# Weight conversions of a second feed-forward moved into the attention, with fewer and larger transfers and a new schedule table

## The chip, the cores and the metric

One core of one Trainium2 chip runs the whole program once. The metric is the device time of that execution in microseconds (us). Engines in the profile: PE is TensorE's matmuls and PEld its weight loads, DVE is VectorE, ACT is ScalarE, POOL is GpSimd, SP is SyncE, which here only issues transfers (SPq in the rows). Each engine works through its own instructions strictly in the order in which they were written.

## The reference

Three stages follow each other, in float32 outside the weights, which come in as float64.

```python
# attention: 4 batches, 8 heads, 576 positions, head size 64
cum = np.cumsum(np.maximum(s, 0.0), axis=-1)
bias = -(cum[:, :, :, None] - cum[:, :, None, :])
scores = np.where(causal, -1000000000.0, scale * q @ k.T + np.minimum(bias, 0.0))
attn = softmax(scores);  x = attn @ v            # then (2304 tokens, 512)
# first feed-forward: d_ff 2048
h = x @ w_in;  g = np.maximum(h, 0.0) + np.log1p(np.exp(-np.abs(h)));  x = g @ w_out
# second feed-forward: d_ff 1536
xn = x / rms * rms_g;  g = xn @ w_gate;  val = xn @ w_val
out = (silu(g) * val) @ w_out
```

## The kernel before

**Weights.** A weight chunk is 128 x 512 float64 values. `w_fetch` loads it raw (512 KB, two raw buffers), `w_conv_a` (ScalarE), `w_conv_d` (VectorE, lines 257 to 262) and `w_conv_p` (GpSimd, line 268) turn its bits into float32. `w_hi` and `w_lo` then split it into a high and a low half, since each product of the feed-forwards is three matmuls (high by high, high by low, low by high; `mm3`). The first feed-forward (ph 1) has 32 chunks, the second (ph 2) 36. `w_store` puts a converted chunk into DRAM (256 KB), `w_load` fetches it back. Of the 68 chunks, 12 of ph 1 are converted and split during the attention. The other 20 of ph 1 and all 36 of ph 2 are converted during the first feed-forward: 24 of the latter are stored, 12 split at once and kept.

**Attention.** 32 heads go in 16 pairs p. For a pair: q and k are loaded (`a_load`), transposed on TensorE (`a_qt`) and split (`a_qh`, `a_ql`). A first pass of scores (`a_one`) gives row maxima on VectorE (`a_m`, line 465), which are transposed (`a_mt`, line 473, once a pair) and sent by a transfer into rows of the operand `aq` (`a_md`, lines 483 and 484). A second pass (`a_two`) makes the transposed scores with the maxima taken off, ScalarE takes exp of them (`a_e`), and `a_v` multiplies by [v | 1], so that 64 rows of the result are the output and the others the row sum. `a_ox` evacuates to xz, `a_zd` moves a sum row into z, `a_zr` makes reciprocals, `a_rd` stores them, `a_rb` broadcasts them into rb, `a_xm` multiplies on GpSimd (line 558) and `a_xw` writes x to DRAM.

**Order.** `attention_ops` lists each of these steps as an operation with an engine, a duration, what it depends on and a period (`base`). `attention_order` ranks them by base x 14 + the table `OFF`, and then repeatedly takes the one that can start first by those durations, the lowest rank first among equals. The result is one order for each engine's instructions. The conversions in it are the operations CF, CA, CD, CP, CH, CL, one chunk each `CONVR` periods. Two of the first feed-forward's products, H0 and H1, are in the same list.

**First feed-forward.** Tokens go in 6 tiles of 384, d_ff in 16 slices f; 96 steps i, the slices 0 to 5 for all tiles first. A step is 12 matmuls for h (`m1_h`), a chain over ScalarE and VectorE (`m1_abs` to `m1_gl`; e, u, l, gh and gl are its tiles), and 12 matmuls for y (`m1_y`). Steps and conversions are placed on one axis by the tables `OFF1` and `OFF2` and sorted. The pool m1 of this stage takes memory that pools of the attention held, so its first tiles wait until those are free. The second feed-forward follows in 72 steps.

Of the kernel before, what the change touches and what calls it, by code (L numbers as in the profile page):

```python
# [45 lines left out]
    "LV": -70.00,  # L46
    "QT0": -54.82,
    "QH0": 10.73,
    "QL0": -43.19,
    "QT1": -41.13,  # L50
    "QH1": -23.99,
    "QL1": -51.10,
    "AQ": -22.67,
    "RA": 33.90,
    "KA": 26.80,
    "RB": 26.23,
    "KB": 49.27,
# [36 lines left out]
    "V11": 21.91,
    "O01": 9.83,
    "O11": 65.74,
    "ZD": -7.14,
    "ZR": -70.00,
    "RS": 24.74,
    "BC": -36.84,  # L100
    "XM": -39.94,
    "XW": 60.21,
    "LD": -44.35,
    "CF": -3.51,
    "CA": -49.20,
    "CD": 59.71,
    "CP": 31.53,
    "CH": -35.20,
    "CL": 63.09,
    "XL": -61.60,  # L110
    "X0": 31.53,
    "X1": 43.56,
    "X2": 45.40,
    "X3": 46.41,
    "H0": -33.34,
    "H1": 19.94,
}
CONV0 = 0.45
CONVR = 1.15
# [34 lines left out]
def attention_moe_kernel(ctx, tc, q, k, v, s, w_in, w_out, w_gate, w_val, w_out2, rms_g, out):  # L154
    nc = tc.nc
# [18 lines left out]
    NA = 2 * FA  # L174
    STEPS = [(t, t, f) for t in range(NTILE) for f in range(FA)]
# [134 lines left out]
    def setup():  # L310
# [3 lines left out]
        for i in range(3):  # L314
            t = pools["nat"].tile([P, NB, 3, D], F32, tag=f"vn{i}", name=f"vn{i}", bufs=1)
# [719 lines left out]
```

## Time and profile before

| | |
|---|---|
| median of 3 runs | 1204.03 us (1203.38 to 1204.65) |
| the profiled execution | 1203.66 us |
| its span, first to last instruction | 1201.9 us |
| PE busy | 1125.2 us, 94% of the span |
| DVE busy | 728.3 us, 61% |
| ACT busy | 543.7 us, 45% |
| POOL busy | 420.2 us, 35% |

The attention takes the first 272 us or so, the first feed-forward the time to about 750 us, the second the rest. The shares are averages over three stages with different limits; what counts is the busy time stage by stage, and which wait ends last there. The rows for that are below.

### The profile page before, as it was taken

How to read it: one execution, taken by the hardware profiler on the slowest of the kernel's cores; microseconds unless marked ns; L12 is line 12 of the kernel's file. 1: busy time of each engine (PE TensorE's matmuls, PEld its weight loads, DVE VectorE, ACT ScalarE, POOL GpSimd, SP SyncE). 2: the span in 40 equal slices, each digit the busy share in tenths (PEclk: the TensorE clock that was granted, in tenths of full speed). 3: DMA queues.
4: the chain of work that ended last, by engine and by line, in shares of the span. 5: the costliest groups of instructions: out<-in, count | busy, mean ns of one | idle time of the engine just before them, and what ended most of it. 6: DMA issues, size and time to landing. Idle time of an engine off the chain costs nothing.

```text
span 1201.9 us, 18473 instructions
## 1 busy us (share of the span) xinstructions
PE 1125.2 (94%) x6884; PEld 1037.3 (86%) x6884; DVE 728.3 (61%) x1208; ACT 543.7 (45%) x1179; POOL 420.2 (35%) x368
## 2 busy tenths in 40 slices
PE   4999999996999989999888889999999999999998
PEld 3788888886988889998887878999999999999997
DVE  5666655415999999989999897343233332333322
ACT  1444544346777777676676756341121211212111
POOL 4434443225644543456667677660000000000000
PEclk9999999997999999999999999999999999999999
DMA  6555543224333345434533233231001010010000
GB/s 141 149 131 136 140 107 101 69 80 126 130 123 123 123 134 182 134 110 157 162 126 126 66 97 118 93 123 41 7 7 40 14 40 7 7 40 14 27 1 27
DMA packets 129018, 107.55 MB, mean 89 GB/s; under 512 B 69056, under 2 KB 114752, under 8 KB 128864
## 3 DMA queue, kind: packets, MB, share of 16 engines
q1 hardware_dynamic: 128896, 106.37, 29.6%
q8 instruction: 54, 0.88, 0.3%
q14 instruction: 36, 0.29, 0.1%
q0 software_dynamic: 32, 0.00, 0.0%
HBM read 80.36 MB, written 25.83 MB: 88 GB/s over the span
## 4 chain that ended last, share of the span: by engine, by line
PE 47%; DVE 23%; ACT 3%; issue 2%; DMA 1%; POOL 0%; DVEq 0%; SPq 0%
DVE gl L779 5%; PE v L727 4%; PE v L728 4%; PE v L729 4%; PE g L729 4%; PE g L728 4%; PE g L727 4%; DVE l L770 4%; DVE e L762 3%; PE o L903 3%; PE o L904 3%; PE o L902 3%; DVE ur L258 2%; DVE e L766 2%; DVE ur L262 2%
## 5 line engine op out<-in xcount | busy, mean ns | idle before, releaser
L268 POOL TENSOR_TENSOR wf<-ur 128x512 int32<-128x512 int32 x68 | 94.6, 1391 | 187.1 <-DVE ur L262 97.4
L728 PE MATMUL y<-gl,w 128*128 128x384 f32 x384 | 135.0, 351 | 25.5 <-DVE gl L779 25.5
L727 PE MATMUL y<-gh,w 128*128 128x384 f32 x384 | 131.7, 343 | 14.8 <-ACT e L746 11.6
L887 DVE TENSOR_TENSOR u<-g,u 128x384 f32<-128x384 f32 x71 | 39.5, 557 | 159.1 <-ACT u L886 159.1
L729 PE MATMUL y<-gh,w 128*128 128x384 f32 x384 | 131.1, 341 | 0.0
L465 DVE TENSOR_REDUCE mc<-s 128x1 f32<-128x128 f32 (+4 forms) x160 | 77.8, 537 | 68.6 <-PE s L451 47.2
L889 ACT ACTIVATE gh<-l 128x384 fp32r<-128x384 f32 x72 | 37.8, 524 | 156.0 <-DVE l L888 156.0
L728 PEld LDWEIGHTS y<-gl,w 128*128 128x128 f32 x384 | 73.6, 192 | 37.3 <-DVE gl L779 37.0
L886 ACT ACTIVATE u<-g 128x384 f32<-128x384 f32 x71 | 34.8, 490 | 151.9 <-PE g L729 151.9
L728 PE MATMUL g<-xl,w 128*128 128x384 f32 x284 | 95.5, 336 | 1.7 <-DVE xl L721 1.7
L779 DVE TENSOR_TENSOR gl<-l,gh 128x384 fp32r<-128x384 f32 x90 | 93.9, 1044 | 4.5 <-ACT gh L774 0.7
L727 PE MATMUL g<-xh,w 128*128 128x384 f32 x284 | 95.7, 337 | 0.7 <-ACT xh L720 0.7
L729 PE MATMUL g<-xh,w 128*128 128x384 f32 x284 | 95.8, 337 | 0.0
L728 PE MATMUL v<-xl,w 128*128 128x384 f32 x284 | 95.6, 337 | 0.0
L727 PE MATMUL v<-xh,w 128*128 128x384 f32 x284 | 95.5, 336 | 0.0
L729 PE MATMUL v<-xh,w 128*128 128x384 f32 x284 | 95.4, 336 | 0.0
L727 PE MATMUL h<-xh,w 128*128 128x384 f32 x256 | 87.5, 342 | 6.3 <-DVE e L766 6.3
L774 ACT ACTIVATE gh<-l 128x384 fp32r<-128x384 f32 x96 | 49.9, 520 | 92.9 <-DVE l L770 92.5
L513 ACT ACTIVATE e<-t 128x448 f32<-128x448 f32 (+2 forms) x128 | 57.2, 502 | 73.9 <-PE t L506 71.9
L728 PE MATMUL h<-xl,w 128*128 128x384 f32 x256 | 86.7, 339 | 3.8 <-POOL xl L724 3.6
L727 PEld LDWEIGHTS y<-gh,w 128*128 128x128 f32 x384 | 73.4, 191 | 17.0 <-ACT e L746 11.9
L762 DVE SCALAR_TENSOR_TENSOR e<-u,e 128x384 f32<-128x384 f32 x96 | 74.4, 775 | 21.1 <-ACT l L754 21.0
(168 smaller groups left out, 3018.2 us busy)
## 6 DMA issues: line engine op xcount, KB each, us to landing
raw<-in_moe_w_out_dram SPq DMA_DIRECT2D x28, 512.0 KB
raw<-in_moe_w_in_dram SPq DMA_DIRECT2D x16, 512.0 KB
raw<-in_moe_w_gate_dram SPq DMA_DIRECT2D x12, 512.0 KB
raw<-in_moe_w_val_dram SPq DMA_DIRECT2D x12, 512.0 KB
wf<-wf SPq DMA_DIRECT2D x24, 256.0 KB
wl<-wf SPq DMA_DIRECT2D x24, 256.0 KB
xr<-x SPq DMA_DIRECT2D x28, 192.0 KB
qn<-in_q_dram SPq DMA_DIRECT2D x32, 144.0 KB
```

Source lines behind the costliest of these rows:

```text
L268: nc.gpsimd.tensor_tensor(out=w.bitcast(I32), in0=u, in1=r3, op=ALU.add)
L465: nc.vector.reduce_max(out=o, in_=x, axis=AX.X, negate=True)
L513: nc.scalar.activation(out=st["e", p, hd][:, c:c + w], in_=st["t", p, bk][hd][:, 0:w], func=AF.Exp)
L727: nc.tensor.matmul(o, wh, xh, start=start, stop=False)
L728: nc.tensor.matmul(o, wh, xl, start=False, stop=False)
L729: nc.tensor.matmul(o, wl, xh, start=False, stop=stop)
L762: nc.vector.scalar_tensor_tensor(out=e, in0=st.pop(("u", i)), scalar=-1.0, in1=e, op0=ALU.add, op1=ALU.subtract)
L770: nc.vector.tensor_tensor(out=l, in0=l, in1=st.pop(("e", i)), op=ALU.add)
L774: nc.scalar.activation(out=gh, in_=st["l", i], func=AF.Copy)
L779: eng.tensor_tensor(out=gl, in0=st.pop(("l", i)), in1=f32(st["gh", i]), op=ALU.subtract)
L887: nc.vector.tensor_tensor(out=u, in0=g, in1=u, op=ALU.mult)
L889: nc.scalar.activation(out=gh, in_=l, func=AF.Copy)
```

## The change

All 36 chunks of the second feed-forward are now fetched, converted and stored during the attention (`CONV`, 48 chunks in all, three in about each period); during the first feed-forward 12 of them are only loaded back (`w_load`) and split. The tile `ur` of a conversion has two buffers in the attention (pool `cur`) in place of one. Transfers are merged: q and k of both heads in one each, maxima in two transfers for four, both sum rows in one, both broadcasts in one. For that both heads' outputs lie on partitions 0 to 63 (v and the ones have changed places for the second head, `vn` has a fourth column block), and `a_xm` is one operation over 64 x 1152 where there were two over 64 x 576. `OFF` has new ranks, and H0 and H1 must stand behind the last conversion. `OFF1` and `OFF2` are as before.

```diff
 OFF = {
-    "LV": -70.00,
+    "LV": -52.67,
...
-CONVR = 1.15
+CONVR = 0.33
...
+    CONV = [(1, c) for c in range(NA)] + [(2, c) for c in range(3 * F2)]
...
     def w_conv_a(ph, c):
-        ur = conv.tile([P, 2, 512], I32, tag="ur", name="ur", bufs=1)
+        pool, n = (conv, 1) if "m1" in pools else (pools["cur"], 2)
+        ur = pool.tile([P, 2, 512], I32, tag="ur", name="ur", bufs=n)
...
     def a_load(p):
-            for hd in range(2):
-                nc.sync.dma_start(out=t[:, :, hd, :], in_=src[b, h + hd].rearrange("(p r) d -> p r d", r=QR))
+            nc.sync.dma_start(out=t, in_=src[b, h:h + 2].rearrange("h (p r) d -> p r h d", r=QR))
...
     def a_md(p):
-        for hd in range(2):
-            r = slice(64 * hd + MR, 64 * hd + MR + 1)
-            nc.sync.dma_start(out=aq[r, 0:512], in_=mt[4 * hd:4 * hd + 4])
-            nc.sync.dma_start(out=aq[r, 512:S], in_=mt[8 + hd:9 + hd, 64:P])
+        r = slice(MR, 64 + MR + 1, 64)
+        nc.sync.dma_start(out=aq[r, 0:512], in_=mt[0:8])
+        nc.sync.dma_start(out=aq[r, 512:S], in_=mt[8:10, 64:P])
...
     def a_zd(p):
-        for hd in range(2):
-            nc.sync.dma_start(out=z[half(hd)], in_=st["xz", p, hd][64 - 64 * hd:65 - 64 * hd, :])
+        nc.sync.dma_start(out=z, in_=st["xz", p][64:65])
...
     def a_rb(p):
-        for hd in range(2):
-            nc.sync.dma_start(out=rb[half(hd)], in_=rdd[p][hd:hd + 1].broadcast_to([64, S]))
+        rb = st["rb", p] = pools["xo"].tile([D, 2, S], F32, tag="rb", name="rb", bufs=2)
+        nc.sync.dma_start(out=rb, in_=rdd[p].unsqueeze(0).broadcast_to([D, 2, S]))
 
     def a_xm(p):
-        for hd in range(2):
-            r = half(hd)
-            nc.gpsimd.tensor_tensor(out=x[r], in0=st.pop(("xz", p, hd))[r], in1=rb[r], op=ALU.mult)
+        x = st["x", p] = pools["xo"].tile([D, 2, S], F32, tag="x", name="x", bufs=2)
+        nc.gpsimd.tensor_tensor(out=x, in0=st.pop(("xz", p))[0:D], in1=st.pop(("rb", p)), op=ALU.mult)
...
-        for c in range(NA):
+        for c, (ph, ch) in enumerate(CONV):
...
-            cv("CA", "ACT", 0.66, w_conv_a, ["CF"] + was("CP", 1))
-            cv("CD", "DVE", 1.65, w_conv_d, ["CA"])
-            cv("CP", "POOL", 1.28, w_conv_p, ["CD"] + was("CL", 3))
-            cv("CH", "POOL", 0.62, w_hi, ["CP"])
-            cv("CL", "POOL", 1.28, w_lo, ["CH"])
+            cv("CA", "ACT", 1.33 if r3_act(ph, ch) else 0.67, w_conv_a, ["CF"] + was("CP", 2))
+            cv("CD", "DVE", 1.55 if r3_act(ph, ch) else 1.98, w_conv_d, ["CA"])
+            cv("CP", "POOL", 1.28, w_conv_p, ["CD"] + ([("CL" if c - 3 < NA else "CS", c - 3)] if c > 2 else []))
+            if ph == 1:
+                cv("CH", "POOL", 0.62, w_hi, ["CP"])
+                cv("CL", "POOL", 1.28, w_lo, ["CH"])
+            else:
+                cv("CS", "SP", 0.4, w_store, ["CP"], lat=2.2)
...
-                    for nm, fn in CONV1 + (SPLIT if ph == 1 or c < NA else (("CS", w_store),)):
+                    for nm, fn in CONV1 + SPLIT if ph == 1 else (("CF", w_load),) + SPLIT if c < NA else ():
```

What the new table does to the order shows in three places. The first is VectorE in the middle of the attention, one pair's worth: L465 (later L467) are row maxima into mc, L408 (L410) the low halves of q and k, L542 and L543 the reciprocals. Before:

```order
L465 TENSOR_REDUCE mc_165<-s 128x1 x4
L465 TENSOR_REDUCE mc_167<-s 128x2 x2
L465 TENSOR_REDUCE mc_167<-s 128x1 x2
L469 TENSOR_TENSOR mc_167<-mc_167 128x2
L465 TENSOR_REDUCE mc_167<-s 128x1 x2
L408 SCALAR_TENSOR_TENSOR hl<-qkT,hl 128x96x4
```

After, with the conversion's three steps L261, L263 and L265 on the tile ur:

```order
L467 TENSOR_REDUCE mc_165<-s 128x1 x4
L261 TENSOR_SCALAR ur<-ur 128x512
L263 TENSOR_SCALAR ur<-ur 128x512
L265 SCALAR_TENSOR_TENSOR ur<-raw,ur 128x512
L467 TENSOR_REDUCE mc_167<-s 128x2 x2
L467 TENSOR_REDUCE mc_167<-s 128x1 x2
L471 TENSOR_TENSOR mc_167<-mc_167 128x2
L261 TENSOR_SCALAR ur<-ur 128x512
L263 TENSOR_SCALAR ur<-ur 128x512
L265 SCALAR_TENSOR_TENSOR ur<-raw,ur 128x512
L467 TENSOR_REDUCE mc_167<-s 128x1 x2
L410 SCALAR_TENSOR_TENSOR hl<-qkT,hl 128x96x4
```

Two conversions now stand between groups of row maxima (a third stands between the low halves of q and those of k).

The second place is SP's queue in the middle of the attention: rd is the store of the reciprocals, rb their broadcast, aq<-mt the maxima, vn the loads of v. Before:

```order
L546 DMA rd_87<-z 128x9
L551 DMA rb<-rd_87 64x576 x2
L483 DMA aq<-mt 1x4x128
L484 DMA aq<-mt 1x16x4
L483 DMA aq<-mt 1x4x128
L484 DMA aq<-mt 1x16x4
L381 DMA vn_150<-in_v_dram 128x4x64 x2
L384 DMA vn_150<-in_v_dram 64x2x64
```

After, with the fetches of raw chunks (L240) and the store of a converted one (L275):

```order
L546 DMA rd_85<-z 128x9
L240 DMA raw<-in_moe_w_gate_dram 128x4x128
L275 DMA wf_113<-wf 128x512
L550 DMA rb<-rd_85 64x1152
L240 DMA raw<-in_moe_w_val_dram 128x4x128
L383 DMA vn_144<-in_v_dram 128x4x64 x2
L386 DMA vn_144<-in_v_dram 64x2x64
L484 DMA aq<-mt 2x4x128
L485 DMA aq<-mt 2x64
```

The maxima's transfers have moved behind a fetch and the loads of v, the broadcast behind a fetch and a store.

The third place is TensorE at the end of the attention: L524 (L525) are the last products with V, L727 to L729 (L726 to L728) the matmuls of h, of which a block has 12. Before:

```order
L727 MATMUL h<-xh,w_659 128x384
L728 MATMUL h<-xl,w_659 128x384
L729 MATMUL h<-xh,w_659 128x384
L524 MATMUL x_3768<-e,vn_144 128x192 x2
L524 MATMUL x_3768<-e,vn_144 128x64
L524 MATMUL x_3768<-e,vn_144 128x192 x2
L524 MATMUL o_3774<-e,vn_144 128x384
L524 MATMUL o_3774<-e,vn_144 128x256
L524 MATMUL o_3774<-e,vn_144 128x128
L727 MATMUL x_3840<-xh,w_945 128x384
```

After:

```order
L525 MATMUL o_4013<-e,vn_144 128x384
L525 MATMUL o_4013<-e,vn_144 128x256
L525 MATMUL o_4013<-e,vn_144 128x128
L525 MATMUL x_4021<-e,vn_144 128x192 x2
L525 MATMUL x_4021<-e,vn_144 128x64
L525 MATMUL x_4021<-e,vn_144 128x192 x2
L726 MATMUL h<-xh,w_569 128x384
L727 MATMUL h<-xl,w_569 128x384
L728 MATMUL h<-xh,w_569 128x384
```

H0 and H1 stood among the last products with V (H0 three of those further up); now both follow the last of them.

## Rows read from the trace of the kernel before

**Rows 1.** Busy time of each engine by stretch (instructions), granted clock, DMA.

```profile
core 0: us, PE busy (x) PEld busy (x) DVE busy (x) ACT busy (x) POOL busy (x), PEclk, DMA share, GB/s
...
40.00:240.00 200.00, 199.84 (x1889) 171.05 (x1888) 120.75 (x276) 93.10 (x240) 80.11 (x71) 1.00 0.45 114
240.00:284.00 44.00, 31.38 (x227) 27.32 (x223) 7.43 (x17) 17.31 (x43) 12.12 (x9) 0.89 0.30 96
284.00:440.00 156.00, 143.26 (x766) 135.33 (x767) 146.37 (x210) 116.36 (x248) 85.32 (x65) 0.98 0.40 127
440.00:480.00 40.00, 40.00 (x231) 39.75 (x230) 37.69 (x62) 31.03 (x66) 12.16 (x11) 1.00 0.50 162
440.00:730.00 290.00, 262.50 (x1441) 251.38 (x1440) 271.98 (x377) 197.89 (x412) 171.65 (x142) 0.99 0.40 128
800.00:1160.00 360.00, 360.00 (x1899) 337.56 (x1898) 114.76 (x213) 72.89 (x149) 7.01 (x5) 1.00 0.08 24
```

**Rows 2.** What PE waited for, 440 to 730 us: total, times, longest.

```profile
PE y L728 <- DVE gl L779: 14.7, 15, 3.4
PE h L727 <- DVE e L766: 5.3, 5, 1.6
PE h L728 <- POOL xl L724: 3.3, 2, 1.7
```

**Rows 3.** One short stretch, columns as in rows 1.

```profile
510.00:513.20 3.20, 3.20 (x11) 3.20 (x12) 3.13 (x6) 2.62 (x6) 1.68 (x2) 0.53 0.60 219
```

**Rows 4.** VectorE's groups, 440 to 730 us: busy us, mean ns, idle before.

```profile
L262 DVE SCALAR_TENSOR_TENSOR ur<-raw,ur 128x512 int32<-128x512 int32 x35 | 26.3, 752 | 1.2
L258 DVE TENSOR_SCALAR ur<-ur 128x512 f32<-128x512 f32 x35 | 23.9, 683 | 4.5 <-ACT ur L248 4.5
...
L260 DVE TENSOR_SCALAR ur<-ur 128x512 int32<-128x512 int32 x35 | 19.5, 558 | 1.2
```

**Rows 5.** The tile ur, 440 to 735 us: ns minimum/median/maximum, first and last start.

```profile
L248 ACT ACTIVATE ur<-raw x35: 644/656/680, 441.3 to 715.5; 128x512 f32<-128x512 f32 x35
...
L258 DVE TENSOR_SCALAR ur<-ur x35: 407/422/1514, 442.5 to 717.3; 128x512 f32<-128x512 f32 x35
...
L268 POOL TENSOR_TENSOR wf<-ur x35: 1272/1440/1612, 445.0 to 720.9; 128x512 int32<-128x512 int32 x35
```

**Rows 6.** VectorE's groups, 40 to 240 us, as rows 4.

```profile
L465 DVE TENSOR_REDUCE mc<-s 128x1 f32<-128x320 f32 (+4 forms) x140 | 68.3, 537 | 57.0 <-PE s L451 45.0 <-PE s L445 11.7
...
L262 DVE SCALAR_TENSOR_TENSOR ur<-raw,ur 128x512 int32<-128x512 int32 x11 | 7.6, 692 | 0.4
...
L258 DVE TENSOR_SCALAR ur<-ur 128x512 f32<-128x512 f32 x11 | 5.7, 522 | 0.3 <-ACT ur L248 0.3
L260 DVE TENSOR_SCALAR ur<-ur 128x512 int32<-128x512 int32 x11 | 5.6, 513 | 0.4
```

**Rows 7.** TensorE's timeline: the maxima's transpose, ten pairs apart (start, duration).

```profile
88.17 0.28 PE L473 MATMUL mT<-ident,mc 128*128 128x128 f32 x1
...
230.64 0.28 PE L473 MATMUL mT<-ident,mc 128*128 128x128 f32 x1
```

**Rows 8.** What SP's queue waited for, 20 to 240 us: total, times, longest.

```profile
SPq L483 <- ACT e L513: 12.7, 11, 3.8
SPq L483 <- ACT mt L477: 11.1, 3, 7.3
```

**Rows 9.** TensorE's timeline near the start; idle time before in brackets.

```profile
28.10 0.71 PE L392 MATMUL qkT<-ident,qn 96*128 96x96 f32 x3 [1.51 <-DMA qn<-in_q_dram]
```

**Rows 10.** TensorE's timeline at the first y.

```profile
284.05 0.66 PE L727 MATMUL y<-gh,w 128*128 128x384 f32 x1 [11.57 <-ACT e L746]
```

**Rows 11.** Timelines of SP, GpSimd and ScalarE at the attention's end.

```profile
272.91 1.10 SPq L551 DMA_DIRECT2D rb<-rd  x2
...
275.92 2.86 POOL L558 TENSOR_TENSOR x<-xz,rb 64x576 f32<-64x576 f32 x2 [5.18 <-DMA rb<-rd]
...
282.70 0.52 ACT L774 ACTIVATE gh<-l 128x384 fp32r<-128x384 f32 x1
```

More of the change, by code (lines that the diff above doesn't have):

```diff
@@ L99 @@
[L99 to L116, printed above, removed]
+    "LV": -52.67,
+    "QT0": -50.26,
+    "QH0": -14.82,
+    "QL0": -1.28,
+    "QT1": 44.67,
+    "QH1": -4.81,
+    "QL1": -59.11,
+    "AQ": -46.37,
+    "RA": -6.41,
@@ new lines @@
+    "KA": 29.15,
+    "RB": -7.55,
+    "KB": -19.97,
+    "RC": -17.34,
+    "KC": 5.02,
+    "RD": -10.66,
+    "MA0": 38.23,
+    "MA1": 27.80,
+    "MB0": -43.48,
+    "MB1": -32.64,
+    "MC0": -10.72,
+    "MC1": -70.00,
+    "MD0": 22.30,
+    "MD1": -60.64,
+    "MN": -60.28,
+    "MT": 22.32,
+    "MH": 2.98,
+    "DM": -70.00,
+    "Ra": -67.80,
+    "Ka": 7.73,
+    "Rb": 8.25,
+    "Kb": 7.75,
+    "Rc": 15.50,
+    "Kc": -27.62,
+    "Rd": 18.00,
+    "Kd": -64.43,
+    "Ea0": -46.31,
@@ new lines @@
+    "Ea1": -20.17,
+    "Eb0": -9.89,
+    "Eb1": 20.86,
+    "Ec0": 24.32,
+    "Ec1": -34.42,
+    "Ed0": 37.23,
+    "Ed1": -12.23,
+    "V00": 42.71,
+    "V10": 53.06,
+    "O00": 22.58,
+    "O10": 56.32,
+    "V01": 68.87,
+    "V11": -47.21,
+    "O01": 28.24,
+    "O11": 23.84,
+    "ZD": -41.28,
+    "ZR": -20.03,
+    "RS": -7.84,
+    "BC": -30.09,
+    "XM": 53.28,
+    "XW": 12.09,
+    "LD": 16.43,
+    "CF": -56.65,
+    "CA": 58.11,
+    "CD": 37.96,
+    "CP": 34.54,
+    "CH": 63.23,
@@ L117 @@
+    "CL": 45.30,
+    "CS": 0.58,
+    "XL": 49.85,
+    "X0": 49.47,
+    "X1": 37.16,
+    "X2": 55.13,
+    "X3": 16.72,
+    "H0": -17.59,
+    "H1": -63.46,
 }
 CONV0 = 0.45
-CONVR = 1.15
+CONVR = 0.33
 OFF2 = {
@@ L384, in a_loadv @@
         nc.sync.dma_start(
-            out=t[64:P, 4, 0:3:2, :], in_=v[b, h:h + 2, 512:S, :].rearrange("h p d -> p h d"))
+            out=t[64:P, 4, 0:4:2, :], in_=v[b, h:h + 2, 512:S, :].rearrange("h p d -> p h d"))
     def a_qt(p, which):
@@ L644, in attention_ops @@
             op((f"H{i}", 0), "PE", 2.1, lambda i=i: m1_h(i),
-               [(f"X{a}", 0) for a in range(KD)] + [("MT", NP - 1), ("CL", NA - 2)] + [("R" + x, p) for x in "abcd" for p in (NP - 2, NP - 1)], NP, mode="f")
+               [(f"X{a}", 0) for a in range(KD)] + [("MT", NP - 1), ("CL", NA - 1), ("CP", len(CONV) - 1)] + [("R" + x, p) for x in "abcd" for p in (NP - 2, NP - 1)], NP, mode="f")
         for o in ops:
@@ L932, in attention_moe_kernel @@
                 make_cum(cp)
-            open_pools(("e", 4), ("sml", 1), ("xo", 1))
+            open_pools(("e", 4), ("sml", 1), ("xo", 1), ("cur", 1))
             for fn in attention_order(attention_ops()):
```

85 lines of the change are left out of this document (15 added, 70 removed).

## The prediction

> **What bounds the kernel now.** I read the stretches first [rows 1]. From 40 to 240 us, the attention, TensorE is busy 199.84 of 200 us, VectorE 120.75, ScalarE 93.10 and GpSimd 80.11: TensorE is the bound and the others have room. From 440 to 730 us, the second part of the first feed-forward, it is the other way round: VectorE is busy 271.98 of 290 us (94%) and TensorE 262.50, with waits in it. The stretch 800 to 1160 us, the second feed-forward, is TensorE alone (360.00 of 360) and the change does not touch it.
>
> How much TensorE loses from 440 to 730 us comes out of one row: in 440 to 480 us it was never idle and ran 231 matmuls, 40.00 / 231 = 0.173 us each. The 1441 matmuls up to 730 us need 1441 x 0.173 = 249.5 us at that pace, and took 290: **40.5 us lost**. The waits say to whom [rows 2]: products with gl (the low half, written by VectorE) 14.7 us, h behind VectorE's e 5.3, h behind GpSimd's xl 3.3. Those three are 23.3 us; much of the other 17 will be the clock. Behind one such wait, from 510 to 513.2 us, the granted clock is 0.53 [rows 3], close to the lower of its two levels (1.2 for 2.4 GHz). A wait that is gone gives this back too.
>
> What VectorE does in that stretch besides the feed-forward is conversion of weights of the second feed-forward: 35 chunks, 23.9 + 26.3 + 19.5 = 69.7 us, 1.99 us a chunk [rows 4].
>
> **The change, part by part.**
>
> *Conversions out of the first feed-forward.* 36 chunks leave it: 36 x 1.99 = 72 us of VectorE, 36 x 2 x 0.656 = 47 us of ScalarE, 36 x 1.44 = 52 us of GpSimd [rows 4, 5], 36 fetches and 24 stores on SP's queue. In 440 to 730 us VectorE is left with 272 - 70 = 202 us, less than the 249.5 of TensorE; ScalarE with 198 - 46 = 152, GpSimd with 172 - 50 = 122. TensorE becomes the bound. Twelve loads of stored chunks come in, 256 KB each, with the same split into halves as before; they take the places of twelve fetches of 512 KB. I leave out of the gain the 3.3 us behind xl, which the conversion does not cause, and about 1 us for evacuations that come earlier now: **-36 us**. From below 20: half of the loss stays, as it would if the length of the chain from h to gl counted and not VectorE's load. From above 40.5. The stretch 284 to 440 us keeps its 20 conversions and so its own loss, 156 - 766 x 0.173 = 23.5 us with VectorE at 94%.
>
> *Conversions into the attention.* What can hide them there: from 40 to 284 us VectorE is idle 79 + 37 = 116 us, ScalarE 107 + 27 = 134, GpSimd 120 + 32 = 152 [rows 1]. To be added on VectorE: 36 x (0.522 + 0.513 + 0.692) = 62 us at the attention's durations [rows 6], 72 at the feed-forward's. That makes VectorE busy 128 + 62 to 72 of 244 us, 78 to 82%, against TensorE's 95%. So on average it is hidden. It isn't on each step, since VectorE takes its rows in order: the order shows about three conversions in each pair, two of them between groups of row maxima, and a conversion that is late makes the next maxima late, then the freeing of a score bank, then TensorE. The pair's period is (230.64 - 88.17) / 10 = 14.25 us [rows 7]; VectorE's share of it rises to about 12. I take 0.3 us a pair, 15 pairs: **+4 us**, bounds 0 (all hidden, as the 11 conversions of this stretch are now) and +20 (below).
>
> How much such a conversion can be held up, the rows show: the same operation, 128x512, has a median of 0.422 us and a maximum of 1.514 [rows 5]; its mean is 0.683 where GpSimd is busy 59% (171.65 of 290), and 0.522 where it is busy 40%. With 36 GpSimd additions more, GpSimd in the attention comes to (80 + 38) / 200 = 59% too, so 1.99 us a chunk is the nearer figure. The Trainium skill, page "SBUF — State Buffer", section "Who interferes with whom", gives a reason: VectorE operations in a two-port mode or with two SBUF inputs share a port pair with GpSimd, and whichever comes second "fully blocks" until the first one ends. By that rule the merged multiplication, one operation where there were two, would shut VectorE out for twice as long, and the sum would go towards the third rival's time; by the mean of 1.99 us it stays where it is. The trace agrees in that the maximum exceeds the median by about the length of one GpSimd operation, 1.091 to 1.44 us; on the merged one no run here shows anything yet.
>
> *Merged transfers.* Per pair the SP queue loses 2 (q, k), 2 (the maxima), 1 (sums) and 1 (reciprocals), 6 issues, and gains 36/16 = 2.25 fetches and as many stores: it gets no longer. Bytes are the same, so the transfers themselves cost what they did: nothing in the steady part, where SP stood waiting for the maxima anyway, 23.8 us in 14 waits [rows 8]. At the start it is worth something: TensorE waits 1.51 us for q [rows 9] while SP issues without a break. **-1 us**, bounds 0 and -3. The added bytes are 36 x 0.79 MB = 28 MB; at 162 GB/s for a DMA share of 0.50 [rows 1] that is 87 us of share, in 244 us +0.36 on 0.42: 0.78, not full.
>
> *New ranks: the end of the attention.* TensorE stands still 11.57 us before the first y [rows 10]. The chain behind it: reciprocals broadcast from 272.91, multiplication on GpSimd 275.92 to 278.78, then e, u, l, gh on ScalarE from 282.70, y at 284.05 [rows 11]. The order shows two h blocks of 12 matmuls between the last products with V; after the change they stand behind all of them. So the last V is done 24 x 0.173 = 4.2 us sooner and the h fill the hole. One broadcast instead of two saves another 0.55 us (half of 1.10). And the first e no longer waits for GpSimd's multiplication but for transfers, so part of the 5.3 us from 278.78 to 284.05 runs beside it; I count 3.3 of it. **-8 us**, bounds -3 (the four last conversions, which now lie in this tail, hold up the evacuations) and -12.
>
> Sum: 1203.66 (the profiled execution's time; its span is 1201.9, and 1.8 lie around it) - 36 + 4 - 1 - 8 = 1162.7, so **1163 us**. The median of the three runs is 0.4 us above the profiled one; that changes nothing at this size.
>
> **Rivals.**
>
> *VectorE becomes a second bound in the attention.* For: 82% of an engine that works in order, three conversions a pair, each of which may lose 1.514 - 0.422 = 1.1 us. 36 x 1.1 = 40 us, half of which reaches TensorE: +20 instead of +4, **1179 us**. Against: before its row maxima VectorE has stood idle 57.0 of 200 us for scores [rows 6], 57.0 x 14.25 / 200 = 4.1 us a pair, and in these gaps the conversions fit.
>
> *The first feed-forward recovers half.* The y products wait for gl at the end of a chain over two engines; if the chain and not VectorE's load were the limit, the gain is 20: **1179 us**. Against: 231 matmuls without a gap from 440 to 480 us, with conversions in it.
>
> *The gain goes back behind the merged multiplication.* If in each chunk one conversion step stood behind a whole multiplication, 2.86 us [rows 11], VectorE would need 128 + 62 + 36 x 2.86 = 293 us in 244: +49 instead of +4, 1208 us; at nine chunks in ten +39, 1198. So **about 1203**, as now. Against: the multiplication runs once a pair and takes a fifth of it, and three chunks cannot all meet it.
>
> *Slower: the maxima's transfer comes late.* Before, it stood right behind the broadcast; now a fetch that waits for VectorE (two raw buffers) and three loads of v that wait for TensorE stand ahead of it on SP. Everything in the second score pass waits for it. SP has 23.8 / 14 = 1.7 us to spare at this place, and two issues fewer. Each us beyond that costs 15 us; from 3 us a pair (45 us) the gain is gone, at 4 us a pair the time is 1163 - 4 + 60 = **1219 us**. Against: v is three buffers deep and SP hardly waits for TensorE at these loads now.
>
> **How the numbers follow.** The forecast's own case 0.63 (1150 to 1176), VectorE second bound 0.18, half recovered 0.09, all given back 0.04, slower 0.06. 0.2% or 2.4 us is about what a measurement of this kernel tells from no change. Faster 0.90, same 0.04, slower 0.06. The range runs from 1150 (1203.66 - 40.5 - 12 - 1, the upper bounds of both gains and nothing lost in the attention) to 1188 (the 1179 of two rivals, and 9 us for both costs in part); it leaves out the last two cases and some of the ends of the others.
>
> **What would show it.** Right: from 440 us on a y every 4.16 us (24 matmuls), VectorE there near 70%; in the attention a period of 14.25 to 14.6 us and no new wait at the score products; at the end of it a hole of under 5 us. Wrong: a period over 15 us, with TensorE behind row maxima (VectorE) or behind the maxima's transfer (SP); or waits for gl that stay though VectorE has room.

## The result

| | before | changed kernel |
|---|---|---|
| median | 1204.19 us (4 runs) | 1211.76 us (1209.59 to 1213.53, 4 runs) |
| ratio | | 1.0063, 95% interval 1.0043 to 1.0082 |
| span of the profiled execution | 1201.9 us | 1210.8 us |

It is slower by 0.6%, where 3.4% faster was forecast. The 8.9 us between the two spans can be laid out along TensorE's timeline:

| stretch | before | after | difference |
|---|---|---|---|
| start to the maxima's transpose of the fifth pair | 88.2 | 96.4 | +8.2 |
| from there to the end of the last product with V | 180.1 | 222.9 | **+42.8** |
| from there to the first y | 15.8 | 18.4 | +2.6 |
| first y to the 34th (the feed-forward's first part, roughly) | 160.7 | 160.2 | -0.5 |
| 34th y to the 93rd | 287.6 | 247.5 | **-40.1** |
| 93rd y to the end | 469.5 | 465.3 | -4.2 |

So the gain came, and the attention took all of it and 9 us more. The stretches of the changed kernel, with the columns of [rows 1]:

```profile
core 0: us, PE busy (x) PEld busy (x) DVE busy (x) ACT busy (x) POOL busy (x), PEclk, DMA share, GB/s
40.00:240.00 200.00, 177.75 (x1544) 147.48 (x1542) 160.89 (x301) 103.30 (x246) 100.12 (x76) 0.96 0.76 193
60.00:100.00 40.00, 35.53 (x329) 30.04 (x327) 38.42 (x67) 21.18 (x53) 28.76 (x24) 1.00 0.66 168
60.00:240.00 180.00, 158.00 (x1381) 130.88 (x1378) 142.93 (x268) 94.35 (x225) 86.04 (x63) 0.95 0.79 198
500.00:745.00 245.00, 245.00 (x1413) 244.67 (x1413) 179.01 (x267) 159.85 (x339) 116.99 (x106) 1.00 0.22 69
```

The last row is what the prediction promised of the feed-forward: TensorE without a gap, 1413 matmuls at 245 / 1413 = 0.173 us, full clock, VectorE at 73%. The first row is the surprise. Against [rows 1] TensorE does 1544 matmuls in 200 us, not 1889, and no other engine is full: VectorE 80%, ScalarE 52%, GpSimd 50%. The DMA share rose from 0.45 to 0.76. What TensorE waited for from 60 to 240 us (engine, tile, line, releaser: us, times, longest):

```profile
PE t L500 <- DVE hl L410: 6.0, 8, 1.0
PE t L500 <- DVE mc L467: 5.2, 3, 2.5
PE o L525 <- ACT xz L534: 4.6, 5, 1.7
PE t L500 <- DMA aq<-mt: 4.6, 4, 1.5
PE x L525 <- ACT e L514: 1.0, 2, 0.6
```

Five kinds of short waits, each on another tile, 21.4 us together, and none that comes in each pair: TensorE's own waits don't name one cause. The rest of the loss is in the busy time: 1381 matmuls are worth 1381 x 199.84 / 1889 = 146 us at the pace of before and took 158. Most of that goes with the clock of 0.95 (0.05 x 158 = 8 us, an estimate).

One pair of SP's queue shows the loop (start, us, line, transfer, count):

```profile
189.71 0.53 SPq L538 DMA_DIRECT2D z<-xz  x1
191.92 0.66 SPq L558 DMA_DIRECT2D x<-x  x1
192.69 0.53 SPq L240 DMA_DIRECT2D raw<-in_moe_w_out_dram  x1
193.31 2.13 SPq L275 DMA_DIRECT2D wf<-wf  x2
195.53 0.66 SPq L376 DMA_DIRECT2D qn<-in_q_dram  x1
196.28 1.07 SPq L376 DMA_DIRECT2D kn<-in_k_dram  x1
197.44 1.77 SPq L546 DMA_DIRECT2D rd<-z  x1
199.32 0.39 SPq L240 DMA_DIRECT2D raw<-in_moe_w_gate_dram  x1
199.80 0.45 SPq L275 DMA_DIRECT2D wf<-wf  x1
203.79 0.49 SPq L550 DMA_DIRECT2D rb<-rd  x1
```

Before, the same place read (one pair of the kernel before, same columns):

```profile
198.94 0.50 SPq L546 DMA_DIRECT2D rd<-z  x1
201.40 1.13 SPq L551 DMA_DIRECT2D rb<-rd  x2
```

GpSimd's multiplications on both sides of these rows in the changed kernel, a conversion behind each of them, and VectorE's reciprocals between them:

```profile
189.27 2.62 POOL L554 TENSOR_TENSOR x<-xz,rb 64x1152 f32<-64x1152 f32 x1 [8.95 <-DMA rb<-rd]
191.85 1.27 POOL L271 TENSOR_TENSOR wf<-ur 128x512 int32<-128x512 int32 x1
...
193.19 0.21 DVE L543 RECIPROCAL z<-z 128x9 f32<-128x9 f32 x1
...
207.61 2.62 POOL L554 TENSOR_TENSOR x<-xz,rb 64x1152 f32<-64x1152 f32 x1 [9.54 <-DMA rb<-rd]
210.20 1.27 POOL L271 TENSOR_TENSOR wf<-ur 128x512 int32<-128x512 int32 x1
```

The reader is to see three things. The reciprocals are ready at 193.40, but their store rd is issued at 197.44, behind two stores of converted chunks and the loads of q and k. It takes 6.3 us until the broadcast that waits for it can go, where it took 2.5; of this rd's own issue holds SP for 1.77 us, 0.50 before, and the rows do not tell for what. And the rows close on themselves: SP issues the store of x (L558) at 191.92, 0.03 us after the multiplication ends, so it stood waiting for it; the transfers behind it follow, rd among them, then the broadcast, then the next multiplication. From one multiplication to the next that is 2.62 + 5.55 + 6.35 + 3.82 = 18.34 us (the multiplication, until rd, until rb, until the next one), about one period.

From the issue of the sum row (z) to the start of the multiplication the mean over the pairs whose z is issued before 240 us (13 before, 10 after) is 10.75 us before and 17.40 us after: 3.07 to 3.96 for z to the reciprocals, 1.56 to 3.69 until SP issues rd, 2.90 to 4.86 until rb, 3.22 to 4.89 until the multiplication.

### The profile page after: what moved, and what is told of

Its sections match the earlier page's. It is cut to its first block, busy times and chain, and to the rows that moved or that the text cites. A ratio compares the mean times of both kernels' runs of the same rounds, so it can differ in the third digit from the quotient of the medians.

```text
span 1210.8 us, 18329 instructions
## 1 busy us (share of the span) xinstructions
PE 1130.1 (93%) x6884; PEld 1045.5 (86%) x6884; DVE 721.8 (60%) x1208; ACT 545.7 (45%) x1179; POOL 410.7 (34%) x352
## 4 chain that ended last, share of the span: by engine, by line
PE 68%; DVE 15%; DMA 6%; issue 5%; POOL 3%; ACT 2%; SPq 1%; POOLq 0%; DVEq 0%; ACTq 0%
PE g L728 4%; PE g L727 4%; PE v L728 4%; PE v L726 4%; PE v L727 4%; PE g L726 4%; PE y L727 4%; PE y L728 4%; PE y L726 4%; PE o L902 3%; PE o L903 3%; PE o L901 3%; PE t L500 3%; PE h L726 2%; PE h L727 2%
## 5 line engine op out<-in xcount | busy, mean ns | idle before, releaser
L727 PE MATMUL y<-gl,w 128*128 128x384 f32 x384 | 130.9, 341 | 12.0 <-DVE gl L778 10.7
L726 PE MATMUL y<-gh,w 128*128 128x384 f32 x384 | 129.2, 336 | 0.4 <-DVE yt L811 0.4
L728 PE MATMUL y<-gh,w 128*128 128x384 f32 x384 | 128.8, 336 | 0.0
L271 POOL TENSOR_TENSOR wf<-ur 128x512 int32<-128x512 int32 x68 | 91.3, 1343 | 88.8 <-DVE ur L265 57.1
L888 ACT ACTIVATE gh<-l 128x384 fp32r<-128x384 f32 x72 | 37.8, 524 | 155.0 <-DVE l L887 155.0
L467 DVE TENSOR_REDUCE mc<-s 128x2 f32<-128x512 f32 (+4 forms) x160 | 77.8, 536 | 34.1 <-PE s L453 23.4
L727 PE MATMUL g<-xl,w 128*128 128x384 f32 x284 | 95.5, 336 | 0.7 <-DVE xl L720 0.7
L726 PE MATMUL h<-xh,w 128*128 128x384 f32 x256 | 87.3, 341 | 9.2 <-DVE e L765 9.2
L728 PE MATMUL g<-xh,w 128*128 128x384 f32 x284 | 95.8, 337 | 0.0
L726 PE MATMUL g<-xh,w 128*128 128x384 f32 x284 | 95.6, 337 | 0.0
L726 PE MATMUL v<-xh,w 128*128 128x384 f32 x284 | 94.9, 334 | 0.0
L728 PE MATMUL v<-xh,w 128*128 128x384 f32 x284 | 94.9, 334 | 0.0
L727 PE MATMUL v<-xl,w 128*128 128x384 f32 x284 | 94.9, 334 | 0.0
L723 POOL TENSOR_TENSOR xl<-xr,xh 128x384 fp32r<-128x384 f32 x44 | 47.8, 1085 | 128.4 <-ACT xh L722 124.8
L727 PEld LDWEIGHTS y<-gl,w 128*128 128x128 f32 x384 | 72.4, 189 | 17.7 <-DVE gl L778 16.0
L727 PE MATMUL h<-xl,w 128*128 128x384 f32 x256 | 87.1, 340 | 0.5 <-POOL xl L723 0.3
L728 PE MATMUL h<-xh,w 128*128 128x384 f32 x256 | 86.5, 338 | 0.0
L554 POOL TENSOR_TENSOR x<-xz,rb 64x1152 f32<-64x1152 f32 x16 | 43.7, 2729 | 115.4 <-DMA rb<-rd 101.3
## 6 DMA issues: line engine op xcount, KB each, us to landing
wf<-wf SPq DMA_DIRECT2D x36, 256.0 KB
wl<-wf SPq DMA_DIRECT2D x36, 256.0 KB
```

The lines of the kernel that those rows point to most:

```text
L467: nc.vector.reduce_max(out=o, in_=x, axis=AX.X, negate=True)
L554: nc.gpsimd.tensor_tensor(out=x, in0=st.pop(("xz", p))[0:D], in1=st.pop(("rb", p)), op=ALU.mult)
L723: eng.tensor_tensor(out=xl, in0=xr, in1=f32(xh), op=ALU.subtract)
L726: nc.tensor.matmul(o, wh, xh, start=start, stop=False)
L727: nc.tensor.matmul(o, wh, xl, start=False, stop=False)
L728: nc.tensor.matmul(o, wl, xh, start=False, stop=stop)
```

## The experiments

The first column to read is the start of the first y: it holds the whole attention (284.1 before, 337.7 after). "34 to 93" is the feed-forward's second part, as above. The period is the mean over eight pairs in the middle. These three columns come from the one profiled execution of each run. Four executions of the changed kernel lie between 1209.59 and 1213.53 us, so differences of a few us in them tell little.

| run | median, us | ratio to before (95%) | period | first y | 34 to 93 |
|---|---|---|---|---|---|
| before | | | 14.2 | 284.1 | 287.6 |
| changed kernel | 1211.76 | 1.0063 (1.0043 to 1.0082) | 18.5 | 337.7 | 247.5 |
| e1_conv_back | 1240.44 | 1.0307 (1.0290 to 1.0325) | 17.2 | 320.3 | 286.5 |
| e2_short_fetch | 1196.64 | 0.9942 (0.9924 to 0.9959) | 17.0 | 322.2 | 247.5 |
| e3_no_dve | 1206.67 | 1.0023 (1.0013 to 1.0033) | 18.1 | 331.1 | 247.5 |
| e4_xm_late | 1227.48 | 1.0206 (1.0191 to 1.0222) | 19.4 | 352.8 | 247.5 |
| e5_same_order | 1205.95 | 1.0024 (1.0015 to 1.0034) | 14.3 | 288.4 | 286.3 |
| e6_xz3 | 1211.44 | 1.0071 (1.0051 to 1.0091) | 18.7 | 338.2 | 247.5 |
| e7_xz3_late | 1226.22 | 1.0191 (1.0157 to 1.0226) | 18.9 | 352.4 | 247.5 |
| e8_merged_only | 1226.69 | 1.0200 (1.0183 to 1.0217) | 15.0 | 303.9 | 287.5 |
| e9_no_stores | 1194.19 | 0.9935 (0.9916 to 0.9954) | 16.7 | 319.6 | 247.5 |
| e10_no_fetch | 1191.13 | 0.9900 (0.9877 to 0.9923) | 16.8 | 315.9 | 247.5 |
| e11_no_transfers | 1173.04 | 0.9742 (0.9719 to 0.9765) | 15.3 | 299.8 | 247.5 |
| e12_half | 1194.89 | 0.9931 (0.9911 to 0.9951) | 16.3 | 312.7 | 256.0 |
| e13_short_both | 1188.08 | 0.9869 (0.9841 to 0.9896) | 16.7 | 313.6 | 247.5 |
| e14_act_queue | 1201.59 | 0.9988 (0.9970 to 1.0005) | 17.2 | 320.5 | 247.5 |
| e15_act_half | 1189.95 | 0.9881 (0.9855 to 0.9906) | 16.2 | 306.1 | 254.5 |
| e16_act_third | 1201.19 | 0.9981 (0.9951 to 1.0010) | 16.5 | 306.6 | 265.2 |
| e17_act_two_thirds | 1189.97 | 0.9891 (0.9849 to 0.9934) | 16.6 | 319.4 | 250.2 |
| e18_act_half_xz3 | 1188.60 | 0.9875 (0.9852 to 0.9897) | 16.1 | 309.7 | 255.0 |

**First set: which part of the change.** Putting the conversions back:

```diff
-CONVR = 0.33
+CONVR = 1.15
-    CONV = [(1, c) for c in range(NA)] + [(2, c) for c in range(3 * F2)]
+    CONV = [(1, c) for c in range(NA)] + [(2, c) for c in range(0)]
...
```

> The changed kernel, but the 36 chunks of the second feed-forward are converted in the first feed-forward again (CONVR 1.15 as before); merged transfers and the new ranks stay. If the added conversions make the attention slow: period back to 14.2 to 14.6 us (from 17.8), last V near 270 us, 60 steps of the first feed-forward as slow as before, total 1196 to 1206 us. If the merged transfers or the new ranks make it slow: period stays above 17 us, the gain of 40 us is lost too, total 1240 to 1255 us.

Measured 1240 us and 17.2 us a period, the second branch. But it convicts nothing: with other operations in its list the scheduler makes another order from the same ranks, and that order waits elsewhere (TensorE for row maxima, 14.4 us in 9 waits from 60 to 240 us). Asked for its own plan of this list, it lays the pairs 17.8 us apart; for the list of the changed kernel 14.8. The run was badly made, and e5 below replaces it.

The fetches with their bytes cut (raw is kept in two tiles that stay):

```diff
+        if ph == 2 and c > 1:
+            raw = raws["keep", c % 2]
+            nc.sync.dma_start(out=raw[0:8], in_=w_out2[0:8])
+            raws[ph, c, "d"] = raw
+            return
```

> The changed kernel, but of the 36 chunks of the second feed-forward only the first two are fetched whole; the other 34 fetches move 32 KB in place of 512 KB into the same two buffers, and all steps of the conversion and all stores stay (their values are then not the weights). If the transfers' load holds up the chain sums, reciprocals, broadcast, multiplication: period 14.3 to 15.5 us, last V 270 to 285, total 1160 to 1178 us. If VectorE's extra work sets the period: it stays 17 us or more, total 1200 to 1212 us.

1196.64 us lies between the branches: the first y came 15.5 us earlier, so the bytes of the fetches matter, and they are not all.

```diff
     def w_conv_d(ph, c):
...
+        if ph == 2:
+            return
```

> The changed kernel without the three VectorE operations of the 36 conversions of the second feed-forward (so their values are not the weights); fetches, ScalarE's and GpSimd's steps and the stores stay in their order. If VectorE's load sets the period: 14.3 to 15 us, total 1160 to 1172 us. If the loop multiplication on GpSimd, next conversion behind it, its store on SP's queue, reciprocals' store behind that, broadcast, next multiplication sets it: 17 us or more, total 1200 to 1212 us.

1206.67 us: without any of the added VectorE work the period is still 18.1. VectorE is not the bound of the steady part; the first y moved by 6.6 us only.

The loop that this set assumed, multiplication, conversion, store, reciprocals' store, was tried by moving one operation (code behind the scheduler that takes XM out of the list and puts it behind the next two CP):

> The changed kernel with one thing moved: on GpSimd each pair's multiplication stands behind the next two conversions instead of ahead of them (and the store of x behind it on SP's queue). If the loop through GpSimd and SP's queue sets the period: it falls from 17.8 to 14.8 to 16 us, total 1168 to 1190 us. If VectorE's load sets it: no change, 1206 to 1215 us. If the transfers' load alone does: a little, 17 to 17.5 us, 1200 to 1208 us.

It got slower, 1227.48 us, outside all three branches. The theory in that form fell. But only the tie from the multiplication over the conversions to their stores was cut: the store of x moved back together with the multiplication, still ahead of rd on SP's queue. ScalarE's evacuations now started 0.03 us after the multiplication of two pairs earlier, each time: they waited for its buffer xz.

**Second set: the reuse of xz, and the order by itself.** The scheduler still sees all conversions, so the order of everything else is kept, but those of the second feed-forward are not issued:

```diff
-                op((nm, c), eng, dur, lambda: fn(ph, ch),
+                op((nm, c), eng, dur, lambda: fn(ph, ch) if ph == 1 else None,
```

> The changed kernel in its own order of all other instructions, but with the 36 conversions of the second feed-forward taken out of the attention and put back into the first feed-forward. Theory now: a loop over two pairs sets the period, first evacuation into xz, sum row, reciprocals, their store, broadcast, multiplication, and then the evacuation into the same xz buffer two pairs later (36 us for two periods of 18); the conversions make it long by their transfers and by their places in the in-order queues. Then the period is 14.3 to 15.2 us, last V at 265 to 280, total 1203 to 1218 us. Rival: the new order is slow of itself; then 17 us or more and 1240 to 1255 us.

1205.95 us, period 14.3: the new order is good, and the conversions make the loss. Its row for 60 to 240 us, columns as above:

```profile
60.00:240.00 180.00, 177.45 (x1659) 150.42 (x1658) 114.98 (x231) 82.32 (x216) 63.79 (x45) 0.98 0.48 107
```

From this run to the changed kernel the first y moves from 288.4 to 337.7: **the conversions cost 49.3 us in the attention**.

```diff
-            st["xz", p] = pools["xo"].tile([P, 2, S], F32, tag="xz", name="xz", bufs=2)
+            st["xz", p] = pools["xo"].tile([P, 2, S], F32, tag="xz", name="xz", bufs=3)
```

> The changed kernel with a third buffer for xz, order kept. If the buffer alone closes the loop: period 14.5 to 15.8 us, total 1165 to 1185 us. If the loop is closed by the order too (the evacuation stands on ScalarE behind a conversion that waits for GpSimd, which has the multiplication ahead of it): period 17 to 18 us, total 1200 to 1213 us. If DMA load or VectorE sets the period: no change either.

> The changed kernel with a third buffer for xz and the multiplication behind the next two conversions on GpSimd. If the loop over xz is the bound and both ties of it are needed: period 14.5 to 16 us, total 1165 to 1192 us. If VectorE or the transfers' load is the bound: 17 us or more, total 1200 to 1215 us.

1211.44 and 1226.22 us, not told apart from the same kernels without the third buffer (1211.76 and 1227.48). The reuse of xz is one place where the late multiplication shows, not what makes it late. That theory fell too.

> The merged transfers and the one multiplication alone: old ranks, 12 conversions in the attention, the second feed-forward's in the first as before. The planner places the first five pairs some 10 us later with it. If merging costs nothing: period 14.2 to 14.5 us as before, total 1203 to 1216 us. If the merged operations lengthen the chain past its bound: period 15 us or more, total 1215 to 1235 us.

1226.69 us and 15.0 us, by its numbers the second branch. But the scheduler's late start is the larger part of it (the fifth transpose at 104.1 us, 88.2 before), and from the tenth on the pairs come 14.2 to 14.3 us apart, as before, with a few of 15 to 17 us ahead of that. As this is another order again, the better evidence on merging is e5: all merged, and 14.3 us.

**Third set: the transfers.** Stores left out, fetches left out, both:

```diff
+        if c == 0:
+            nc.sync.dma_start(out=wfd[ph - 1][0], in_=w)
...
+        if ph == 2 and c > 1:
+            raws[ph, c, "d"] = raws["keep", c % 2]
+            return
```

> The changed kernel with the stores of the converted chunks left out, but for the first (all later loads read that one back, so the weights are wrong). Theories left after the xz buffer fell: S, SP's queue in its order (fetches that wait for VectorE and stores that wait for GpSimd hold up the reciprocals' store, the maxima and the broadcast); D, the load of the DMA engines; E, the work on GpSimd, ScalarE and VectorE in its order. S: period 15 to 16.5 us, total 1175 to 1195 us. D: a tenth of the transfer time goes, 17 to 17.5 us, 1200 to 1208 us. E: no change, 1207 to 1213 us.

> The changed kernel with 34 of the 36 fetches of the second feed-forward left out altogether (the conversions work on the first two chunks' data; the weights are wrong), stores kept. S: clearly faster than the run with the short fetches, 14.3 to 15.5 us a period, total 1160 to 1178 us. D: like the short fetches, 1190 to 1200 us. E: 1200 us or more.

> Both left out, fetches and stores of the second feed-forward's conversions; only their work on ScalarE, VectorE and GpSimd stays in the attention (the weights are wrong). S or D: period 14.3 to 14.8 us, total 1160 to 1172 us. E: 16.5 us or more, total 1190 us or more.

The first y comes 18.1, 21.8 and 37.9 us earlier. With no transfers, and all the work of the conversions still on the three engines, the total is 1173.04 us, 10 us above the forecast. TensorE and VectorE then read, for 60 to 240 us:

```profile
60.00:240.00 180.00, 172.32 (x1565) 144.57 (x1563) 157.13 (x305) 110.15 (x261) 100.34 (x72) 0.98 0.49 112
```

VectorE is busy 157.13 of 180 us, more than in the changed kernel, and TensorE does 1565 matmuls, not 1381. Neither S nor D alone gave these numbers: without stores (1194.19) the total lies at the upper end of S, without fetches (1191.13) in D, without both 1 us above the range of S or D. E alone is out. The two single removals add up to nearly the double one, 39.9 against 37.9 us.

**Fourth set: bytes or places.** One run keeps each issue with its waits and cuts the bytes of both kinds (fetches as in e2, `wfd[ph - 1][c][0:8]` for the stores). The other keeps the bytes and takes the issues off SP's queue:

```diff
-        nc.sync.dma_start(out=dst, in_=src)
+        (nc.scalar if ph == 2 and "m1" not in pools else nc.sync).dma_start(out=dst, in_=src)
...
+        for c in range(NA, len(CONV)):
+            behind(("CF", c), ("CA", c - 1), ("CD", c - 2))
+            behind(("CS", c), ("CP", c), ("CA", c + 2))
```

> The changed kernel in its order with every fetch and store of the second feed-forward's conversions still issued on SP's queue at its place, with its waits, but with 32 KB (fetch) and 16 KB (store) moved in place of 512 and 256 KB (the weights are wrong). If the bytes are what costs (the load of the DMA engines delays the small transfers): like the run without these transfers, 1170 to 1178 us, period 14.3 to 15.2 us. If SP's queue order costs, the fetches that wait for VectorE and the stores that wait for GpSimd: 1182 to 1195 us, period 15.5 to 17 us.

> The changed kernel with all its bytes, but these fetches and stores are issued from ScalarE's queue (fetch c behind the ScalarE step of chunk c-1, store c behind that of c+2, which waits for GpSimd's step of c anyway), so that nothing stands behind them on SP's queue, neither an issue nor a small transfer. If the order of one queue costs: period 14.5 to 15.8 us, total 1170 to 1190 us. If the bytes cost in whatever queue: 17 us or more, total 1200 to 1215 us.

Windows of 60 to 240 us, first e13:

```profile
60.00:240.00 180.00, 165.36 (x1459) 137.62 (x1456) 155.23 (x285) 100.45 (x242) 92.92 (x67) 0.96 0.53 115
```

then e14:

```profile
60.00:240.00 180.00, 160.10 (x1426) 132.03 (x1427) 147.52 (x279) 99.28 (x234) 85.50 (x64) 0.97 0.82 206
```

By these expectations e13 (1188.08 us, 16.7) speaks for the queue's order and e14 (1201.59 us, 17.2) for the bytes: both cost. The first y: 288.4 without conversions (e5), 299.8 with their engine work (e11), 313.6 with the issues too (e13), 337.7 with the bytes. So **11.4 us are engine work, 13.8 the places and waits on SP's queue, 24.1 the bytes**. The medians of the whole runs give 15.0 and 23.7 for the last two. From the other side, taking the places away and leaving the bytes (e14), the first y came 17.2 us earlier. But 4.7 of these lie behind the last product with V, and 5.2 go again in the first part of the feed-forward (165.4 us, 160.2 in the changed kernel). By the totals it is 10.2 us.

The chain from z to the multiplication grows too: 11.52 us in e5, 11.84 in e11, 14.97 in e13, 17.40 in the changed kernel. The engine work, then, does not cost through it: 0.3 us more chain, 1.0 us more period. Moving the issues did not make the transfers themselves quicker: from rd to rb it took 5.61 us in e14, 4.86 in the changed kernel. The Trainium skill, page "DMA: Bandwidth & Descriptors", section "Issuing engines are not separate DMA queues", says so: transfers started by several engines run on the same 16 DMA engines, and only the time to initiate them is saved. It calls that time usually small relative to the transfer itself. Here initiating alone held SP for 0.50 us a fetch and 0.53 a store (100 to 240 us of the changed kernel), 3.1 us a pair for three of each. For 36 chunks that is 37 us, so part of it falls into time in which SP would have waited anyway; the 13.8 us are what these and the waits of the issues cost together.

**Fifth set: how many.** Every second chunk in the attention, in the order of the changed kernel, on SP's queue and on ScalarE's; then every third, and two of three:

```diff
-                op((nm, c), eng, dur, lambda: fn(ph, ch),
+                op((nm, c), eng, dur, lambda: fn(ph, ch) if ph == 1 or ch in KEEP else None,
...
+    KEEP = range(0, 3 * F2, 2)
```

> The changed kernel in its own order, but only every second chunk of the second feed-forward (18) is converted in the attention, the other 18 in the first feed-forward. If the cost in the attention grows with each conversion alike (49 us for 36): last V at 295, total 1203 to 1210 us. If it begins only where the queue or the transfers are full: last V at 272 to 282, total 1183 to 1198 us, faster than both kernels.

> The same queue change with only every second chunk (18) converted in the attention. If the order of one queue costs: last V at 272 to 285, total 1172 to 1188 us. If the bytes cost: like the half run on SP's queue, 1192 to 1198 us.

> As the run with half of the conversions on ScalarE's queue (1190 us), but with every third chunk (12) converted in the attention. 18 chunks cost 18 us there and gave 33 us in the first feed-forward's second part. If each chunk costs and gives alike: last V at 282, total 1193 to 1197 us. If the first chunks cost less than they give, and the last more: 1183 to 1190 us.

> The same with two of three chunks (24). If each chunk costs and gives alike: last V at 294, total 1190 to 1194 us; if the gain is used up by 18 chunks (33 of 40 us) and the cost goes on: 1194 to 1200 us.

On SP's queue (e12, 1194.89 us) the total falls in the second branch and the last V (294.4) in the first. e15 lies between its branches (1189.95, last V 288.1). e17's total (1189.97) is at the lower edge of its first branch, with the last V at 300.7. On ScalarE's queue, for 0, 12, 18, 24 and 36 chunks, the first y stands at 288.4, 306.6, 306.1, 319.4 and 320.5, and the stretch 34 to 93 takes 286.3, 265.2, 254.5, 250.2 and 247.5. Neither goes evenly with the count: the first 18 chunks bring 31.8 of the 38.8 us, and the first 12 already cost 18.2. My expectations for 12 were wrong in both branches (1201.19 us, its ten executions between 1193.97 and 1206.97). In that run ScalarE waited above all for the buffer of the evacuation:

```profile
ACT xz L535 <- POOL x L555: 45.7, 8, 6.7
```

> The run with half of the conversions on ScalarE's queue (1190 us), with a third buffer for xz. In the run with a third of them ScalarE's evacuation waited 45.7 us in 8 times for the multiplication, that is for its buffer. If that reuse is what binds once there are few conversions: last V at 272 to 282 (from 288), total 1176 to 1185 us. If not, as with all 36: 1187 to 1193 us.

1188.60 us with the third buffer, 1189.95 without: no difference that these runs tell apart, so what holds the pairs up with few conversions stays open. Half of the conversions on ScalarE's queue is the version that I would keep of these: 0.9881 (0.9855 to 0.9906) of the time before. e17 and e18 can't be told from it.

## Why the prediction was wrong

**First feed-forward, -36 us: right.** 40.1 us in the stretch, near the upper bound of 40.5. Another 4.7 came outside it (0.5 ahead, 4.2 behind), which the sum had not priced, so some 45 in all, above the bound. The waits behind gl went with the conversions. That much of the other 17 us was the clock does not hold: over 440 to 730 us the granted clock is 0.99 [rows 1], about 3 us of 290.

**Conversions into the attention, +4 us, bounds 0 and +20: the step that failed.** It measured +49.3. I priced 62 to 72 us of VectorE work against VectorE's idle time and asked only whether an engine is full. For that part the bounds held: all engine work costs 11.4 us (e11), nearly three times the +4, and VectorE's operations 6.6 (e3). What was missing is the 37.9 us of the transfers, which the sum put at nothing. Two sentences of the prediction let them go. "SP's queue gets no longer" counts issues, and not what each waits for in an in-order queue, with the reciprocals' store, the broadcast and the maxima behind it. SP's three longest waits in the steady part of the changed kernel, 100 to 240 us:

```profile
SPq L550 <- DMA rd<-z: 15.7, 6, 3.5
SPq L558 <- POOL x L554: 13.6, 7, 2.8
SPq L275 <- POOL wf L271: 9.1, 8, 2.6
```

The same stretch before, its two longest:

```profile
SPq L551 <- DMA rd<-z: 20.8, 10, 2.8
SPq L483 <- ACT e L513: 11.9, 10, 3.8
```

The wait of the broadcast for rd is no new one ([rows 8] does not show it). New are the waits for GpSimd, of the store of x and of the converted chunks' stores, 22.7 us. In e5, without the added conversions, that for x is 0.7 us. The fetches' wait for VectorE is long too, 29.3 us from 20 to 240, but nearly all of it lies ahead of 100 us, and 19.6 us of it are in e5 as well: it is not what the added transfers cost.

And "0.78, not full" is a share, which says how much fits and nothing of how long a small transfer takes beside large ones: from rd to rb 2.90 us before at a share of 0.45, 3.90 in e13 at 0.53, 4.86 in the changed kernel at 0.79. The share was also set against the wrong time: the steady part has three fetches and stores in a pair, not 36 / 16 = 2.25, and 0.79 x 18.1 = 14.3 us of all DMA engines in each pair (18.1 us a pair from the fifth to the fourteenth: (259.5 - 96.4) / 9). At a period of 14.25 us that would be a share of 1.0, an estimate; a share of 1 is no fixed end, short stretches read up to 1.14 (last section).

**Start, -1 us: wrong,** +8.2, and +8.6 in e5, so it is the new order and not the added chunks. Two things go with it. The wait for q that was to go got longer: 4.22 us, and 1.51 before [rows 9], and the first maxima's transpose already comes 6.2 us later. And 12 conversions of the first feed-forward now fall into the first four pairs, with VectorE busy 38.42 of 40 us from 60 to 100 us (25.32 before). The second is the first rival, VectorE as second bound, in one place. No run parts the two. I had not looked at the order there.

**End, -8 us, bounds -3 and -12: half.** In e5, from the fifth transpose to the first y, it is 191.6 us against 195.9 before, -4.3. The last V comes 6.6 us sooner and the first y then 2.3 us later behind it. The h blocks stand in the hole, but in the changed kernel 8.17 us of it stay idle (11.57 before, under 5 forecast), for its end is set by the chain behind the last V and not by TensorE: 12.6 us from the last V to the end of the last multiplication (10.5 before), and the first l waits for it, since its pool takes that memory:

```profile
331.91 0.52 ACT L753 ACTIVATE l<-e 128x384 f32<-128x384 f32 x1 [2.86 <-POOL x L554]
```

Two slips in the working change nothing here: 282.70 us in [rows 11] is the start of gh alone (e starts at 278.81), and the low end of the range takes the start at -1, not at its bound of -3.

**The rivals.** VectorE as the second bound of the whole attention falls with e3, the half recovery with the 40.1 us. The maxima's late transfer was the one on the slow side. It is there, from transpose to issue 2.76 us after and 0.71 before, but 1.98 in e5, where it costs no period, and 2.05 in e13, where TensorE does not wait for it. In the changed kernel it waits 4.6 us for it in 180: a small part, and one that comes with the bytes. The multiplication that shuts VectorE out happens too: the longest of 31 operations whose median is 693 ns lasted 3132, that is 2.44 us more, about one merged multiplication of 2.62, which started 0.04 us ahead of it. Before, the longest delay was 1.08 in the attention and 1.09 in the feed-forward [rows 5]. This agrees with the rule of the Trainium skill's page "SBUF — State Buffer", section "Who interferes with whom", that whichever of the two comes second waits out the whole instruction of the first. But the VectorE work as a whole is worth 6.6 us here.

**Shown and open.** Shown: the conversions cost the attention 49.3 us, of which the bytes are about 24, the places on SP's queue about 14, the engine work about 11, each within a few us. The split also depends on the order in which the parts are taken away.

Read from the traces, and cut by no run: the loop over SP's queue, multiplication, store of x, rd behind it, broadcast, next multiplication. In the changed kernel the store of x is issued 0.03 to 0.07 us behind the end of nine multiplications on end (135 to 277 us), and rd goes 2.1 to 4.4 us after its reciprocals are ready in seven of these pairs. Before, the store of x came 1.0 to 5.5 us behind the multiplication in the same nine pairs: SP did not wait for it, the loop was open. Without the added transfers' bytes and issues (e11) it is open again, 0.9 us or more; in e14 it is closed, 0.03 us in all nine. (In e5 it is 0.03 us in three of the nine at a period of 14.3, so the wait of that store alone doesn't make a pair long.) The run that would test it, rd ahead of the store of x, is missing; e4 and e7 moved that store later. In the runs in the changed kernel's order the chain from z to the multiplication gets longer with the period, roughly. In e1, another order, it is 9.58 us at a period of 17.2, so there something else sets the period.

A second path stands untested beside it. ScalarE takes its steps of the conversion in order with the exps and the evacuations, and from 60 to 240 us of the changed kernel it waits 44.6 us for them, before not at all:

```profile
ACT ur L251 <- POOL wf L271: 26.3, 8, 4.1
ACT ur L251 <- DMA raw<-in_moe_w_gate_dram: 10.4, 6, 2.1
ACT ur L251 <- DMA raw<-in_moe_w_out_dram: 7.9, 6, 2.0
```

With short transfers (e13) the waits for raw nearly go (0.9 us), those for GpSimd stay (25.2). How much of the 24 and the 14 us goes by this path, no run says.

## What to carry to other kernels

Work moved under another stage brings its transfers with it: price the DMA time of a period against that period, and every wait that an issue puts into an in-order queue against what stands behind it, before asking whether an engine has room. Where a chain with several small dependent transfers closes once a period, look for its slack (here 1.0 to 1.7 us in six pairs before) and not at the engines' idle time alone; this is argued from the traces. And move a part: half of the conversions brought four fifths of the feed-forward's gain.

## What the hardware showed

A stall can cost twice, though not each does. In the changed kernel TensorE was busy 2.48 us of 140 to 144 us, and the granted clock stayed 1.00 in the 4 us behind it. It was busy 2.56 us of 208 to 212 us, and from 212 to 220 us its granted clock is 0.50, the lower of its two levels (1.2 for 2.4 GHz):

```profile
140.00:144.00 4.00, 2.48 (x18) 1.89 (x19) 3.93 (x8) 3.06 (x8) 2.29 (x2) 1.00 0.99 272
144.00:148.00 4.00, 4.00 (x52) 3.69 (x49) 3.16 (x7) 2.57 (x7) 0.07 (x1) 1.00 1.14 233
...
208.00:212.00 4.00, 2.56 (x27) 2.14 (x26) 2.02 (x5) 0.50 (x1) 4.00 (x3) 0.99 0.58 117
212.00:216.00 4.00, 3.60 (x14) 2.35 (x12) 3.71 (x7) 2.76 (x8) 2.30 (x3) 0.50 0.98 301
216.00:220.00 4.00, 4.00 (x37) 3.93 (x38) 2.40 (x6) 1.64 (x4) 0.41 (x1) 0.50 1.10 211
```

The last two columns are the DMA share and GB/s. The share can read above 1: 1.14 at 233 GB/s, 0.98 at 301.
